# Attention and expert layer on one core: 2304-byte loads, row-tiled matmuls and a fixed matmul order

## Chip, cores, metric

One core of a Trainium2 chip. The metric is device time in microseconds (us) of one execution of the whole kernel, as the median of several runs. Each execution on record is classed as fast or slow; all that are compared below are fast, unless said otherwise.

Engines: PE does matmuls, DVE is the vector engine, ACT the scalar engine, POOL the third element-wise engine (it also issues the weight loads), SP issues loads and stores. In the kernel before, ACT and POOL issue the loads of k and v as well, and ACT one store. (In both kernels the matmuls write to PSUM and all other tiles lie in SBUF; an evacuation copies a result from the first to the second.)

## The reference, cut to what matters

```python
# q, k, v: (8 batches, 8 heads, 576 tokens, 64), fp32
q_s = softmax of q over the 64 features           # exp, row sum, divide
k_s = softmax of k over the 576 tokens
kv  = einsum('bhsd,bhse->bhde', k_s, v)           # 64 x 64 per head
x   = einsum('bhsd,bhde->bhse', q_s, kv)          # then (batch, 576, 512)
# expert layer: ONE expert per batch, out of 8
logits = x.mean(axis=1) @ w_gate                  # needs all of x of a batch
e      = argmax(logits);  gate = softmax(logits)[e]
out    = gate * (relu(x @ w1[e]) @ w2[e])         # 512 -> 1024 -> 512
```

The choice of the expert needs the mean over all tokens of a batch, so a batch's weights can be asked for only once its attention is done. Both kernels therefore run the attention two batches ahead of the expert layer ("MoE" below).

## The kernel before

The parts that the change and the argument touch:

```python
# loads: 512 tokens as 4 tokens a partition (1024-byte pieces), 64 tokens as a tail (256-byte pieces)
q_main = q[:, :, 0:SM, :].rearrange("b h (p j) d -> b p h (j d)", p=128)
q_tail = q[:, :, SM:S, :].rearrange("b h p d -> b p h d")
...
for hp in range(NP):                     # 4 pairs of heads a batch
    ... 5 transposes of q into PSUM, one copy: qt_sb[feature, token]
    ... 5 matmuls ek x v -> pa[:, 0:128];  5 matmuls ek x ones -> pa[:, 128:129]
    nc.vector.reciprocal(out=icv, in_=pa[:, 128:129])
    nc.vector.scalar_tensor_tensor(out=kv_sb, in0=pa[:, 0:128], scalar=icv, in1=blkmask, ...)
    nc.tensor.matmul(pm, lhsT=kv_sb, rhs=qt_sb[:, 0:SM], start=True, stop=True)
    nc.vector.tensor_tensor_reduce(      # the evacuation of x: PSUM fp32 -> SBUF fp16, and the sum over tokens
        out=xt[:, hp, 0:SM], in0=pm, in1=ones_f32.to_broadcast([128, SM]),
        scale=1.0, scalar=0.0, op0=ALU.mult, op1=ALU.add, accum_out=pooled[:, hp:hp + 1],
    )
    ... the same for the 64-token tail
...
# MoE: 8 hidden chunks (4 matmuls N=512, 4 of N=64, relu on ACT or DVE), then 5 output tiles
#      (8 matmuls each, scaled by gate on ACT or DVE), one store of 4 tiles and one of the tail
for b in range(B + LOOKAHEAD):
    if b < B:
        attention_and_gating(b)
    if b >= LOOKAHEAD:
        moe(b - LOOKAHEAD)
```

The softmax here doesn't subtract the row's maximum and nothing guards it: scores larger than these inputs give would overflow.

## Time and profile before

| | before |
|---|---|
| time, median | 249.94 us (249.49 to 252.18, 3 runs) |
| span of the profiled run | 248.0 us |
| PE busy, DVE busy | 194.3 us, 141.3 us |
| first MoE matmul | 54.0 us |
| one MoE without attention beside it | 17.0 us |

The prediction below shows the slices, the chain and the cost rows of this profile. One line of the page that it only quotes in part, the transfers:

```profile
DMA packets 56863, 50.03 MB, mean 202 GB/s; under 512 B 14352, under 2 KB 55312, under 8 KB 55824
```

Nearly all packets are under 2 KB and a quarter are under 512 B: that is what the change set out to improve.

### The profile page before, as it was taken

To read this page: it belongs to the slowest core of one execution; us is meant where nothing else is said; L and a number is where in the kernel's file an instruction comes from. 1 tells how busy PE (TensorE), PEld (TensorE's weight loads), DVE (VectorE), ACT (ScalarE), POOL (GpSimd) and SP (SyncE) were. 2 spreads that over 40 slices of the span, in tenths; PEclk is the share of its full clock that TensorE was granted. 3 is DMA by queue.
4 is the path that set the end of the run, shared out by engine and by line. 5 is a ranking of instruction groups with operands and counts; after the bars stand their busy time and mean duration, and the time that the engine had idled before them with its cause. 6 is when DMAs were issued, how large, how long until landed. Compare 5 with 4: busy or idle time off the path is not lost.

```text
span 248.0 us, 3617 instructions
## 1 busy us (share of the span) xinstructions
PE 194.3 (78%) x1376; PEld 100.3 (40%) x1376; DVE 141.3 (57%) x397; ACT 80.6 (32%) x106; POOL 41.1 (17%) x62
## 2 busy tenths in 40 slices
PE   0006645129954999999999999999999999999862
PEld 0004323015522554555545455554545444444321
DVE  0067998606890799698798699547465422222120
ACT  2083705004600650652651563123122322413311
POOL 2040020502040204213304021301400500000000
PEclk9999999999996899999999999999999999999999
DMA  6999999999999699999999999994894398105005
GB/s 193 249 259 298 271 286 250 269 242 205 275 273 207 113 278 244 259 233 290 271 247 204 201 299 176 155 199 181 141 206 185 48 204 237 45 0 190 0 0 190
DMA packets 56863, 50.03 MB, mean 202 GB/s; under 512 B 14352, under 2 KB 55312, under 8 KB 55824
## 3 DMA queue, kind: packets, MB, share of 16 engines
q0 software_dynamic: 29440, 21.50, 57.7%
q1 hardware_dynamic: 14224, 17.84, 22.6%
q10 hardware_dynamic: 13184, 10.49, 15.3%
q8 instruction: 10, 0.16, 0.2%
q14 instruction: 5, 0.04, 0.1%
HBM read 61.88 MB, written 9.44 MB: 288 GB/s over the span
## 4 chain that ended last, share of the span: by engine, by line
PE 60%; DMA 18%; DVE 15%; ACT 2%; issue 2%; POOLq 1%; POOL 1%; SPq 0%; DVEq 0%
PE po L277 24%; PE phm L252 19%; DMA w_sb<-in_moe_w_dram 13%; DMA qm<-in_q_dram 5%; PE pa L159 4%; DVE qs L117 4%; PE pa L145 3%; DVE eq L120 3%; DVE xt L188 3%; PE pht L257 2%; PE pa L168 2%; PE pa L163 2%; PE pm L185 2%; DVE hsb L264 1%; PE pa L150 1%
## 5 line engine op out<-in xcount | busy, mean ns | idle before, releaser
L252 PE MATMUL phm<-xt,w_sb 128*128 128x512 f16 x256 | 71.3, 392 | 16.8 <-DMA w_sb<-in_moe_w_dram 15.6
L277 PE MATMUL po<-w_sb,hsb 128*128 128x512 f16 (+1 forms) x320 | 77.8, 380 | 3.3 <-DVE osb L284 1.7
L277 PEld LDWEIGHTS <-hsb 128*128 128x128 f16 (+1 forms) x320 | 30.6, 100 | 39.5 <-issue 8.1
L262 ACT ACTIVATE hsb<-phm 128x512 f16<-128x512 f32 x32 | 19.1, 596 | 55.8 <-PE phm L252 55.5
L252 PEld LDWEIGHTS <-w_sb 128*128 128x128 f16 x256 | 21.7, 99 | 38.2 <-DMA w_sb<-in_moe_w_dram 16.7
L282 ACT ACTIVATE osb<-po,gate 128x512 f32<-128x512 f32 (+1 forms) x24 | 16.4, 684 | 63.4 <-PE po L277 63.4
L145 PE MATMUL pa<-ident,eq 128*128 128x128 f16 x128 | 14.9, 245 | 22.4 <-DVE eq L120 20.3
L264 DVE TENSOR_SCALAR hsb<-phm 128x512 f16<-128x512 f32 x32 | 22.0, 686 | 15.7 <-PE phm L252 15.4
L284 DVE TENSOR_SCALAR osb<-po,gate 128x512 f32<-128x512 f32 x16 | 12.0, 748 | 29.1 <-PE po L277 29.1
L117 DVE TENSOR_REDUCE qs<-eq 128x32 f32<-128x2048 f16 x8 | 18.2, 2276 | 14.6 <-ACT eq L108 14.6
L188 DVE CUSTOM_DVE_ANT_0 xt<-pm,ones_f 128x512 f16<-128x512 f32 x32 | 21.4, 687 | 5.8 <-PE pm L185 5.1
L178 DVE RECIPROCAL icv<-pa 128x1 f32<-128x1 f32 x32 | 5.1, 164 | 28.1 <-PE pa L172 27.9
L145 PEld LDWEIGHTS <-eq 128*128 128x128 f16 x128 | 9.5, 108 | 27.7 <-DVE eq L120 20.3
L108 ACT ACTIVATE eq<-qm 128x2048 f16<-128x2048 f32 x8 | 15.3, 1910 | 15.9 <-DMA qm<-in_q_dram 9.0
L110 ACT ACTIVATE ek<-km 128x2048 f16<-128x2048 f32 x8 | 15.2, 1904 | 11.6 <-DMA km<-in_k_dram 10.6
L120 DVE TENSOR_TENSOR eq<-eq,qsi 128x2048 f16<-128x2048 f16 x8 | 18.2, 2276 | 0.0
L98 POOL DMA_DIRECT2D vm<-in_v_dram x8 | 7.3, 910 | 63.2 <-PE pa L163 62.8
L257 PEld LDWEIGHTS <-w_sb 128*128 128x128 f16 x256 | 13.0, 101 | 8.3 <-issue 0.6
L185 PE MATMUL pm<-qt_sb,kv_sb 128*128 128x512 f16 x32 | 12.9, 423 | 4.3 <-DVE kv_sb L180 4.3
L159 PE MATMUL pa<-vm,ek 128*128 128x128 f16 x128 | 14.7, 243 | 1.5 <-DVE qt_sb L156 1.5
L156 DVE COPY qt_sb<-pa 128x576 f16<-128x576 f16 x32 | 14.0, 450 | 3.2 <-PE pa L150 3.0
L257 PE MATMUL pht<-xt,w_sb 128*128 128x64 f16 x256 | 14.7, 197 | 0.0
(52 smaller groups left out, 168.7 us busy)
## 6 DMA issues: line engine op xcount, KB each, us to landing
w_sb<-in_moe_w_dram POOLq DMA_DIRECT2D x32, 512.0 KB, 11.9
km<-in_k_dram ACTq DMA_DIRECT2D x8, 1024.0 KB, 9.9
qm<-in_q_dram SPq DMA_DIRECT2D x8, 1024.0 KB, 13.3
out_dram<-osb SPq DMA_DIRECT2D x8, 1024.0 KB, 6.2
vm<-in_v_dram POOLq DMA_DIRECT2D x8, 512.0 KB, 13.2
qtl<-in_q_dram SPq DMA_DIRECT2D x8, 128.0 KB, 11.0
ktl<-in_k_dram ACTq DMA_DIRECT2D x8, 128.0 KB, 9.5
out_dram<-osb ACTq DMA_DIRECT2D x8, 128.0 KB, 3.5
```

Source lines behind the costliest of these rows:

```text
L117: nc.vector.tensor_reduce(out=qs, in_=eq, op=ALU.add, axis=AX.X)
L120: nc.vector.tensor_tensor(out=eq, in0=eq, in1=qsi.unsqueeze(3).to_broadcast([128, 4, H, Dh]), op=ALU.mult,)
L145: nc.tensor.transpose(out=qT_ps[:, j * 128:(j + 1) * 128], in_=eq[:, j, hs, :], identity=ident,)
L159: nc.tensor.matmul(pa[:, 0:128], lhsT=ek[:, j, hs, :], rhs=vm[:, hs, j, :], start=(j == 0), stop=False,)
L185: nc.tensor.matmul(pm, lhsT=kv_sb, rhs=qt_sb[:, 0:SM], start=True, stop=True)
L188: nc.vector.tensor_tensor_reduce(out=xt[:, hp, 0:SM], in0=pm, in1=ones_f32.to_broadcast([128, SM]), scale=1.0, scalar=0.0, op0=ALU.mult, o ...
L252: nc.tensor.matmul(phm, lhsT=w1_sb[:, dc, fsl], rhs=xt[:, dc, 0:SM], start=(dc == 0), stop=(dc == ND - 1),)
L257: nc.tensor.matmul(pht[:, fc, :], lhsT=w1_sb[:, dc, fsl], rhs=xt[:, dc, SM:S], start=(fc == 0 and dc == 0), stop=(fc == NF - 1 and dc == N ...
L262: nc.scalar.activation(out=hsb[:, fc, 0:SM], in_=phm, func=AF.Relu)
L264: nc.vector.tensor_single_scalar(out=hsb[:, fc, 0:SM], in_=phm, scalar=0.0, op=ALU.max)
L277: nc.tensor.matmul(po[0:nparts, :], lhsT=hsb[:, fc, cols], rhs=w2_sb[:, fc, :], start=(fc == 0), stop=(fc == NF - 1),)
L282: nc.scalar.mul(osb[0:nparts, st, :], po[0:nparts, :], gate[0:nparts])
```

## The change

Intent: larger descriptors for q, k and v (64 partitions per head with 9 neighbouring tokens each, 9 x 64 x 4 = 2304 bytes), so no token tail in the attention; two heads side by side in the upper and lower 64 rows of PE (row tiles); the column sum of k as an extra ones column of v instead of extra matmuls; gating on one partition; and a Python generator for the attention, stepped once after each step of the MoE, which fixes the order of the matmuls by hand. The core of the diff, with cuts:

```diff
-        qm = qk_in.tile([128, H, 4 * Dh], FP32, name="qm")
-        nc.sync.dma_start(out=qm, in_=q_main[b])
-        ... k on the ACT queue, v on the POOL queue with a cast, three tails
+    def pair_src(t, b, i):
+        return t[b].rearrange("(i n g) (p j) d -> i (g p) n (j d)", i=2, n=2, p=64)[i]
+    def loads(b):
+        for i in range(2):
+            for name, t in (("q", q), ("k", k), ("v", v)):
+                nc.sync.dma_start(out=x, in_=pair_src(t, b, i))      # 2304-byte pieces
 ...
+            for j in range(J):                                       # J = 9
+                for g in range(2):
+                    r = slice(64 * g, 64 * g + 64)
+                    nc.tensor.matmul(kps[g][:, 0:129], lhsT=ek[r, j], rhs=va[r, j], ...)
 ...
-            nc.vector.tensor_tensor_reduce(
-                out=xt[:, hp, 0:SM], in0=pm,
-                in1=ones_f32.to_broadcast([128, SM]), ...
+                xo = xt[:, c, :].rearrange("q (p j) -> q j p", j=J)
+                nc.vector.tensor_tensor_reduce(
+                    out=xo[:, 0:8, :], in0=px.rearrange("q (j p) -> q j p", j=8),
+                    in1=ones_f32.unsqueeze(2).to_broadcast([128, 8, 64]), ...
 ...
-            if st % 2 == 0:
-                nc.scalar.mul(osb...)      # else on DVE
-        nc.sync.dma_start(out=out_main[b], in_=osb[:, 0:4, :])
+            osb = o_pool.tile([128, D], FP32, name="osb")            # 4 buffers
+            nc.scalar.mul(osb[0:rows], po[0:rows], gate[0:rows])
+            nc.sync.dma_start(out=out[b, st * 128:st * 128 + rows, :], in_=osb[0:rows])
 ...
+    with tc.manual_schedule(engines={ET.PE}):
+        for b in range(B):
+            att = attention(n, ins.pop(n), False)                    # n = b + 2
+            next(att)                                                # the preparation
+            for step, _ in enumerate(moe(b)):
+                next(att, None)
+            drain(att)
```

The matmuls leave x in PSUM in the order "for each j, all 64 p", where the token is 9p + j. The new `xo` puts the tokens back in order while it evacuates: neighbouring elements of the input go to places 9 fp16 elements, that is 18 bytes, apart.

## The prediction

> **What bounds the kernel now.** I read the page first (busy shares, the 40 slices, the chain, the groups), then the table of stretches, then VectorE's timeline in a dense stretch. The slices and the chain split the run in two parts:
>
> ```profile
> PE   0006645129954999999999999999999999999862
> DMA  6999999999999699999999999994894398105005
> PE 60%; DMA 18%; DVE 15%; ACT 2%; issue 2%; POOLq 1%; POOL 1%; SPq 0%; DVEq 0%
> ```
>
> A slice is 6.2 us. Until slice 12 (about 78 us) the tensor engine (PE) has holes and DMA is full; from there to the end PE is full and DMA empties out by slice 28. The chain, in order of time, names the holes: whole stretches waiting for expert weights.
>
> ```profile
> 1.34 11.52 DMA qm<-in_q_dram
> 43.33 10.60 DMA w_sb<-in_moe_w_dram
> 69.29 8.30 DMA w_sb<-in_moe_w_dram
> 115.06 14.10 DMA w_sb<-in_moe_w_dram
> ```
>
> (Start, length, what.) The first MoE matmul runs at 54 us. The stretches below give PE's work; columns are window, length, busy us and instructions of PE, weight loads, DVE, ACT, POOL, then clock, DMA share, GB/s written.
>
> ```profile
> 126.00:131.00 5.00, 4.53 (x30) 2.34 (x29) 4.92 (x15) 2.79 (x7) 0.76 (x2) 1.00 1.24 207
> 150.30:173.00 22.70, 22.18 (x169) 11.61 (x168) 14.78 (x54) 5.32 (x10) 3.79 (x6) 1.00 0.99 180
> 214.10:231.10 17.00, 16.99 (x105) 7.89 (x104) 4.30 (x7) 5.05 (x9) 0.00 (x0) 1.00 0.19 70
> ```
>
> A batch has 1376/8 = 172 matmuls, 104 of them MoE. A MoE alone takes 17.0 us (last line); with one batch of attention mixed in about 22 us (middle line). The first line is the weight stream alone: 207 GB/s written as fp16, so 414 GB/s read as fp32, with DMA engines full. Vector-engine costs come from these groups and this piece of timeline:
>
> ```profile
> L188 DVE CUSTOM_DVE_ANT_0 xt<-pm,ones_f 128x512 f16<-128x512 f32 x32 | 21.4, 687 | 5.8 <-PE pm L185 5.1
> L117 DVE TENSOR_REDUCE qs<-eq 128x32 f32<-128x2048 f16 x8 | 18.2, 2276 | 14.6 <-ACT eq L108 14.6
> L120 DVE TENSOR_TENSOR eq<-eq,qsi 128x2048 f16<-128x2048 f16 x8 | 18.2, 2276 | 0.0
> L156 DVE COPY qt_sb<-pa 128x576 f16<-128x576 f16 x32 | 14.0, 450 | 3.2 <-PE pa L150 3.0
> L264 DVE TENSOR_SCALAR hsb<-phm 128x512 f16<-128x512 f32 x32 | 22.0, 686 | 15.7 <-PE phm L252 15.4
> 107.63 0.68 DVE L264 TENSOR_SCALAR hsb<-phm 128x512 f16<-128x512 f32 x1
> 108.25 0.69 DVE L188 CUSTOM_DVE_ANT_0 xt<-pm,ones_f 128x512 f16<-128x512 f32 x1
> 108.87 0.08 DVE L188 DVE_READ_ACCUMULATOR2_ANT pooled<- 128x1 f32 x1
> ```
>
> Independent operations follow 0.62 us apart where one lasts 0.69: I use start-to-start costs.
>
> **What the Trainium skill says.** (1) "TensorE: Matmul & The Clock Gate", back-to-back issue gap: N=512 costs 215.7 ns warm. The trace agrees: 8 po matmuls in 1.73 us on the chain. (2) "TensorEngine Tiling (Array Packing)", key properties: row tiles run in parallel, but switching the mode drains the array; the kernel before has no row tiling, so its trace cannot say what the drain costs. (3) "DMA: Bandwidth & Descriptors", queues, rings and completion order: a ring is consumed in order and an engine alternates between the rings that have work. The trace before has queues 0, 1 and 10 active together, which fits; it gives no shares, so equal shares below are my assumption. (4) The same page, why small descriptors are slow: a fixed cost per packet. Here 14352 of 56863 packets are under 512 B (the 256 B tails).
>
> **The change part by part.**
>
> DMA. Bytes read from HBM are unchanged (61.88 MB). q, k and v go from 1024 B and 256 B pieces to 2304 B, all on the SP queue; v is cast on POOL. Lone load stretches before reach 320 to 360 GB/s; estimate for 2304 B: 390. All 28.3 MB of q/k/v then need 73 us, weights 33.5 MB/414 = 81 us, output 9.4 MB/390 = 24 us: 178 us. DMA alone no longer sets the end if it is fed evenly.
>
> PE per batch of attention: before 20 transposes, 20 kv, 20 column-sum and 8 x matmuls, 22 - 17 = 5 us. After: 36 transposes of N=64 (the N=64 pht matmuls run 30 ns apart: 1.1 us, or half if row tiles overlap), 36 kv of N=129 (at 56 ns 2 us, or 1), x 4 x 0.25 = 1 us, gate 0.5 us: 3 to 4.5 us. The gain is 1 to 2 us a batch, 8 to 16 us in all if PE stays the bound.
>
> Vector engine. Same elements, so the same sum, but the built program's instruction order confines it. Each batch's attention is spread over MoE steps 0 to 9: transposes after hidden chunk 0, kv after 1, x after 2 and 3, the second half at 4 to 7, gate after the first output step. DVE's static order in a half is: 2 copies, hsb, next batch's row-sum and scaling mixed with icv and kv, x evacuations, another hsb. Start-to-start: copies 0.94, hsb 2 x 0.62, row-sum and scaling 2 x 1.23 (2.18 x 1152/2048), icv, reciprocal and kv 1.0, xt 2 x 0.62, tails 0.5: 7.4 us, two halves a batch. The PE needs 4 us of hidden-chunk work per half, so DVE sets the pace of this phase. And in the output phase (5 steps of 1.73 us) DVE has almost nothing: osb moved wholly to ACT, and the next transposes come only after it. Period: 1.75 (chunk, transposes, latency) + 7.4 + 0.8 (second transposes, DVE waiting) + 5.7 (second half up to the evacuation before the last x) + 0.3 + 1.8 (first output step) + 0.6 (gate) + 7.0 = 25.4 us, against 22 before. Six such batches: 152 us, 20 us worse than before. The last two MoEs: 2 x 16.7 = 33 us.
>
> Start. q of a half is 0.59 MB and lands near 5 us instead of 12.9. Both first batches' attention is drained on PE before the first MoE. DVE in order does 7 row-sum and scaling pairs (17 us), four attention halves (4 us each), gates and waits: first MoE at about 43 us instead of 54. Its w1 starts at 28 us and, with half the bandwidth, lands at 40.
>
> A new wait. On SP, the loads of six batches (36 DMAs) stand before the first output, and ACT's fifth output tile reuses the first of 4 osb buffers. That store is behind 21.2 MB of loads in one ring, which by my account share with weights from 28 us on and finish at 80 to 88 us. The first MoE ends near 69 us; ACT, blocked on its osb, cannot evacuate the next MoE. Cost 8 to 18 us, take 14. Later stores follow few loads: none.
>
> End: osb 0.7 and store 3.5 us, as before: 4.
>
> Sum: 43 + 152 + 14 + 33 + 4 = 246. Summing latencies I did not see (mode drains, cold PE at the start) I add 2: 248 us.
>
> **The rivals.** (a) PE stays the bound: the period is 17 + 3.5 = 20.5 us, the load stall is small: 43 + 123 + 33 + 4 + 5 = 208 to 215. For it: DVE was only 57% busy, and the matmul order leaves a chunk between each producer and consumer. Against: the static DVE order, 15 us of work that must fit where PE needs 11. If the period lies between, 225 to 235. (b) The stall behind the loads is the largest: DMA is shared less kindly, the second MoE resumes at 92 us, each period takes 27 us: 262 or more. For it: DMA share is above 1 in all early stretches. Against: fewer packets. (c) DMA stays the bound: 8.9 MB a batch at 400 GB/s is 22 us, less than my period, so it would be hidden; only with a period of 20 us does it bite, and then it gives about 215. (d) POOL's v copies delay weight issues, since they stand before them in its order; weights are asked for over one period ahead, so I expect nothing after the start.
>
> **Range and chances.** My own sum is near the old time with an error of some 12 us: six times the uncertainty of the period (1.5 us) and 8 us of the stall. A rebuild with this much hand-placing suggests somebody saw matmul holes close, so I give the fast side more than the sum does: 228 to 264, faster by over 2% (under 245) 0.42, within 2% 0.31, slower 0.27.
>
> **What would show it right or wrong.** Right: the first MoE matmul at 40 to 46 us; a hole in PE of 8 us or more between 65 and 92 us with ACT's osb waiting for DMA; then a repeating pattern of 25 us with DVE nearly full for 15 us and empty for 8, PE waiting for DVE (hm, tk or x banks) in the hidden-chunk phase; two last MoEs of 16.7 us; DMA far from full after 110 us. Wrong: PE above 95% busy between 45 us and the end, a period near 20 us, or DMA landings of weights in the late chain. The load rate is wrong if q tiles land slower than every 5 us early on.

## The result

The changed kernel took 295.55 us (median of 4 runs, 294.0 to 296.1), the kernel before in the same rounds 249.72 us (248.8 to 252.18). The ratio is 1.179, with a 95% interval of 1.170 to 1.187: slower by 18%, far outside the predicted range. (Ratios here are the mean time of one kernel's fast runs over that of the other's in the same rounds, so not quite the ratio of the medians quoted.)

| | before | after |
|---|---|---|
| time, median | 249.72 | 295.55 |
| span of the profiled run | 248.0 | 292.3 |
| PE busy / DVE busy | 194.3 / 141.3 | 194.8 / 180.7 |
| first MoE matmul | 54.0 | 57.85 |
| DMA packets | 56863 | 31956 |

The page of the changed kernel: busy times, the slices (7.3 us each) of PE, DVE and DMA, the transfers, and the chain by engine.

```profile
PE 194.8 (67%) x1552; PEld 97.3 (33%) x1552; DVE 180.7 (62%) x365; ACT 91.5 (31%) x130; POOL 52.6 (18%) x73
PE   0232233294769566895969585893879675999994
DVE  2699999758870979259870979259571868030210
DMA  7999999999938996499738910497018900696112
DMA packets 31956, 54.81 MB, mean 187 GB/s; under 512 B 2752, under 2 KB 10944, under 8 KB 31936
DVE 52%; PE 42%; DMA 2%; issue 1%; ACT 1%; ACTq 1%; DVEq 0%
```

DVE's share of the chain went from 15% to 52%, and DMA's from 18% to 2%. DVE has 39.4 us more of busy time with fewer instructions. DVE runs at 7 to 9 tenths and then drops to 2, again and again; PE is full for a slice at a time only, until the last ones. (The first line gives each engine's busy us, its share of the span and its instructions.) In the groups of the page one row stands out:

```profile
L182 DVE CUSTOM_DVE_ANT_1 xt<-x,ones_f 128x512 f16<-128x512 f32 x24 | 58.8, 2449 | 2.5 <-PE tk L180 2.5
L187 DVE CUSTOM_DVE_ANT_0 xt<-tk,ones_f,pooled 128x64 f16<-128x64 f32 x32 | 15.9, 513 | 2.2
```

(Busy us and mean ns after the first bar.) This is the evacuation of x. The row of the kernel before, shown in the prediction, had the same 128x512 elements at 687 ns; now it is 2449 ns (2512 ns in the 8 that run before the first MoE), and the 64-token rest went from 278 to 513 ns. The other DVE work of the attention did not get dearer than counted, except for the relu right after the first evacuation of a half (0.83 us from start to start, 0.60 in experiment 2 below). DVE's timeline in one half of a batch's attention (start, length, what):

```profile
94.39 0.82 DVE L154 COPY qt<-tk 128x576 f16<-128x576 f16 x2 [6.69 <-PE tk L147]
...
99.23 2.39 DVE L182 CUSTOM_DVE_ANT_1 xt<-x,ones_f 128x512 f16<-128x512 f32 x1
...
101.23 0.91 DVE L254 TENSOR_SCALAR hsb<-hm 128x512 f16<-128x512 f32 x1
102.06 0.49 DVE L187 CUSTOM_DVE_ANT_0 xt<-tk,ones_f,pooled 128x64 f16<-128x64 f32 x1
...
102.25 2.54 DVE L182 CUSTOM_DVE_ANT_1 xt<-x,ones_f 128x512 f16<-128x512 f32 x1
...
104.95 0.50 DVE L187 CUSTOM_DVE_ANT_0 xt<-tk,ones_f,pooled 128x64 f16<-128x64 f32 x1
```

From the first copy to the end of the last evacuation it is 11.06 us, where the prediction had 7.4. Of this, the piece from the start of the first evacuation (99.23) to the end of the second tail (105.45) is 6.22 us. And PE waits for it (the bracket has the idle time before, and what ended it):

```profile
101.68 0.38 PE L179 MATMUL x<-qt,kv 128*128 128x512 f16 x1 [2.43 <-DVE pooled L182]
...
105.50 0.64 PE L147 MATMUL tk<-ident,eq 64*128 64x64 f16 x17 [2.31 <-DVE pooled L187]
106.07 1.89 PE L242 MATMUL hm<-xt,w_sb 128*128 128x512 f16 x4
```

The table of stretches for one repeat of the pattern, from one MoE's first matmul to the next one's (columns as in the prediction: window, length, busy us and instructions of PE, weight loads, DVE, ACT, POOL, then clock, DMA share, GB/s):

```profile
125.82:158.81 32.99, 25.57 (x195) 12.46 (x195) 22.42 (x45) 11.27 (x16) 6.23 (x8) 0.84 0.84 208
254.67:271.37 16.70, 16.70 (x106) 7.91 (x105) 2.77 (x4) 6.42 (x10) 0.00 (x0) 1.00 0.86 188
```

A batch takes 33.0 us, 16.3 us more than a MoE alone (second line). PE is idle for 7.4 us of it (32.99 - 25.57), and in the trace DVE ends every one of these holes. The clock column of 0.84 is a side effect: after the hole of 2.3 us in front of a transpose (105.50 in the timeline above), the next four 512-wide matmuls took 1.89 us instead of 1.04.

So the mechanism that the prediction chose is there (DVE's fixed order sets the pace while hidden chunks run), but one of its terms is more than three times its predicted size. Why does the same operation on the same number of elements take 3.6 times as long? Three readings:

- The step: fp16 elements written 18 bytes apart are slow to write.
- The form: a three-dimensional access pattern or this operation's variant is slow (the name ends in 1 instead of 0).
- The company: other engines or DMAs disturb the write; in the kernel before they would do less of that.

The Trainium skill has a note that bears on the first, and I had not read it before predicting: the page "SBUF — State Buffer", section "Door 1: The DMA port swizzle", speaks of 16-byte lines and says "each access that crosses to a new line pays a penalty"; it gives 8 bf16 elements as the step that is still free. A step of 9 is just past that, so the page would have warned. It names no size for the penalty.

### The profile page after: what moved, and what is told of

Same layout as the page of the kernel before. It is cut to its first block, busy times and chain, and to the rows that moved or that the text cites. A ratio compares the mean times of both kernels' runs of the same rounds, so it can differ in the third digit from the quotient of the medians.

```text
span 292.3 us, 4145 instructions
## 1 busy us (share of the span) xinstructions
PE 194.8 (67%) x1552; PEld 97.3 (33%) x1552; DVE 180.7 (62%) x365; ACT 91.5 (31%) x130; POOL 52.6 (18%) x73
## 2 busy tenths in 40 slices
DMA packets 31956, 54.81 MB, mean 187 GB/s; under 512 B 2752, under 2 KB 10944, under 8 KB 31936
## 4 chain that ended last, share of the span: by engine, by line
DVE 52%; PE 42%; DMA 2%; issue 1%; ACT 1%; ACTq 1%; DVEq 0%
DVE xt L182 25%; PE po L263 21%; PE hm L242 14%; DVE eq L134 7%; DVE qs L131 6%; DVE xt L187 5%; DVE hsb L254 4%; DMA wg_sb<-in_moe_w_gate_dram 2%; PE tk L147 2%; DVE kv L170 2%; PE ht L247 1%; PE tk L161 1%; DVE qt L154 1%; DVE qsi L133 1%; ACTq L86 1%
## 5 line engine op out<-in xcount | busy, mean ns | idle before, releaser
L242 PE MATMUL hm<-xt,w_sb 128*128 128x512 f16 x256 | 76.4, 430 | 0.0
L182 DVE CUSTOM_DVE_ANT_1 xt<-x,ones_f 128x512 f16<-128x512 f32 x24 | 58.8, 2449 | 2.5 <-PE tk L180 2.5
L254 DVE TENSOR_SCALAR hsb<-hm 128x512 f16<-128x512 f32 x32 | 24.4, 764 | 32.3 <-PE hm L242 32.0
L210 POOL DMA_DIRECT2D w_sb<-in_moe_w_dram x32 | 19.3, 623 | 109.9 <-DVE gt L224 70.7
L252 ACT ACTIVATE hsb<-hm 128x512 f16<-128x512 f32 x32 | 19.0, 593 | 61.9 <-PE hm L242 61.9
L126 POOL CAST va<-v_in 128x1152 f16<-128x1152 f32 x16 | 20.2, 1272 | 89.8 <-PE tk L161 47.8
L131 DVE TENSOR_REDUCE qs<-eq 128x18 f32<-128x1152 f16 x16 | 21.5, 1342 | 7.2 <-ACT eq L115 7.2
L120 ACT ACTIVATE ek<-k_in 128x1152 f16<-128x1152 f32 x16 | 18.5, 1159 | 17.0 <-PE tk L161 16.3
L115 ACT ACTIVATE eq<-q_in 128x1152 f16<-128x1152 f32 x16 | 18.6, 1162 | 16.3 <-PE tk L147 8.1
L134 DVE TENSOR_TENSOR eq<-eq,qsi 128x1152 f16<-128x1152 f16 x16 | 21.7, 1358 | 0.1
L247 PE MATMUL ht<-xt,w_sb 128*128 128x64 f16 x256 | 19.5, 202 | 0.0
L182 DVE CUSTOM_DVE_ANT_1 xt<-po,ones_f 128x512 f16<-128x512 f32 x8 | 18.6, 2512 | 0.7 <-PE po L179 0.4
```

What stands on the lines that cost most here:

```text
L126: nc.gpsimd.tensor_copy(out=va[:, :, 1:].rearrange("p j (n d) -> p n j d", n=2), in_=tiles["v", i].rearrange("p n (j d) -> p n j d", j=J),)
L131: nc.vector.tensor_reduce(out=qs, in_=eq, op=ALU.add, axis=AX.X)
L134: nc.vector.tensor_tensor(out=eq, in0=eq, in1=qsi.unsqueeze(3).to_broadcast([128, J, 2, Dh]), op=ALU.mult,)
L182: nc.vector.tensor_tensor_reduce(out=xo[:, 0:8, :], in0=px.rearrange("q (j p) -> q j p", j=8), in1=ones_f32.unsqueeze(2).to_broadcast([128 ...
L210: nc.gpsimd.dma_start(out=w1_sb[64 * h:64 * h + 64, 2 * i:2 * i + 2, :], in_=w1_src[i, h])
L242: nc.tensor.matmul(phm, lhsT=w1_sb[:, c, fsl], rhs=xt[:, c, 0:SM], start=(c == 0), stop=(c == ND - 1),)
```

## The experiments

### 1. The write made contiguous, rows put in order by the store (e1_contig)

```diff
-                xo = xt[:, c, :].rearrange("q (p j) -> q j p", j=J)
+                xo = xt[:, c, :].rearrange("q (j p) -> q j p", j=J)
...
-            nc.sync.dma_start(out=out[b, st * 128:st * 128 + rows, :], in_=osb[0:rows])
+            for t in range(rows // 64):      # out_jp = out.rearrange("b (p j) d -> b j p d", j=J)
+                nc.sync.dma_start(out=out_jp[b, 2 * st + t], in_=osb[64 * t:64 * t + 64])
```

The access pattern keeps its three dimensions and the operation its name; only the step of the output goes from 18 to 2 bytes. Nine stores of 64 rows a batch take the place of five.

> The changed kernel with one thing undone: xt is written with unit stride (columns in j, p order), and nine stores per batch put the rows back in token order; the result stays right. Theory 1 (the 18-byte step of the 2-byte writes is what made the x evacuations 2.45 us instead of 0.69, and nothing else of importance was mis-sized): the 512-wide evacuation falls to about 0.69 us, the tail from 0.51 to 0.28, the pattern of 33.0 us shrinks to 25 to 26.5, the first MoE matmul moves from 57.9 to 42 to 46 us, and the time is 238 to 255 us; a hole with ACT's osb waiting for a store of up to 18 us may now appear between 65 and 92 us, since the first MoE ends earlier. Theory 2 (the evacuation is slow for another reason, such as its PSUM read, its accumulator[...]): evacuations stay above 1.5 us and the time above 275 us. Theory 3 (other waits between PE and DVE are as large as the evacuations): evacuations fall to 0.69 us but the period stays above 29 us and the time above 265 us.

Measured: 249.84 us (249.4 to 249.91), before 250.05; ratio 0.997 (0.990 to 1.003). The evacuation fell to 685 to 687 ns, still under the name ending in 1. The form is thereby refuted as the cause. The first MoE started at 45.5 us, the pattern was 24.9 us, and a wait of 19.8 us of ACT for an output store appeared, which the changed kernel did not have.

### 2. The stride alone undone (e8_stride_only)

Only the first line of the diff above, with the changed kernel's own five stores. The output rows then stand in another order.

> The changed kernel with the stride of the x write alone undone, and its own two kinds of store kept (five of 128 or 64 rows a batch); the rows of the output then stand in another order, wrong on purpose. It tells whether the stall of the first contiguous run (20 us of ACT waiting for an output store) came from its nine smaller stores or from the loads that stand before any store. Theory R (loads before stores in one ring, the predicted wait): 244 to 253 us, ratio 0.98 to 1.01, one wait of ACT for an output store of 15 to 22 us at 70 to 92 us, pattern 24.5 to 25.5 us. Theory N (the nine small stores made the stall): wait under 5 us, 226 to 236 us, ratio 0.91 to 0.95. Theory S (something else than the stride made the changed kernel slow): over 270 us.

Measured: 249.35 us (248.29 to 250.0), before 250.75 (one of its seven runs is slow and not used in the ratio); ratio 0.998 (0.989 to 1.007). So one line of the change is worth 46 us (295.55 to 249.35), and the nine smaller stores of the first experiment cost nothing that these runs can resolve (249.84 against 249.35). DVE's timeline in the same half as above, ACT's at the end of the first MoE, and the stretch of one repeat:

```profile
117.10 0.82 DVE L154 COPY qt<-tk 128x576 f16<-128x576 f16 x2 [6.70 <-PE tk L147]
...
121.94 0.68 DVE L182 CUSTOM_DVE_ANT_1 xt<-x,ones_f 128x512 f16<-128x512 f32 x1
...
124.19 0.28 DVE L187 CUSTOM_DVE_ANT_0 xt<-tk,ones_f,pooled 128x64 f16<-128x64 f32 x1
```

```profile
69.23 0.69 ACT L268 ACTIVATE osb<-po,gate 128x512 f32<-128x512 f32 x1 [1.04 <-PE po L263]
90.61 0.68 ACT L268 ACTIVATE osb<-po,gate 64x512 f32<-64x512 f32 x1 [20.70 <-DMA out_dram<-osb]
```

```profile
115.55:140.45 24.90, 21.75 (x195) 10.99 (x195) 15.06 (x45) 11.15 (x16) 6.23 (x8) 1.00 1.05 275
```

From the first copy to the end of the tail it is 7.37 us, against 7.4 in the prediction and 11.06 in the changed kernel; the evacuations' own piece is 2.53 us instead of 6.22. That is 3.7 us a half, 7.4 us a batch, of the 8.1 us by which the patterns differ (33.0 and 24.9). In the second fence the fifth output tile waits 20.7 us for a buffer, whose store stands behind the loads: SP issued it at 69.3 us, and it landed at 90.5, right after the last of the loads issued before it (89.1). It is the wait that the prediction had put at 8 to 18 us. Theory R held in all its numbers.

The trace also shows what sets the repeat. PE is idle for 3.15 us of it (24.90 - 21.75), in five holes, and DVE ends all five. A repeat in which DVE has two row sums and scalings of the next batch to do takes 24.9 us, the fifth, with one of them left, 23.2, and the sixth, with none, 21.6.

A warning on correctness: the comparison with the reference passed this output too, as it passed the next experiment's, although both have their rows in another order. Its tolerance does not see the order of rows. That the versions called right below store their rows in order rests on the index argument (place 64j + p of x holds token 9p + j, and the stores undo that), not on the comparison.

### 3. The stride alone added to the kernel before (e3_before_strided)

```diff
+            xo = xt[:, hp, :].rearrange("q (p j) -> q j p", j=9)
             nc.vector.tensor_tensor_reduce(
-                out=xt[:, hp, 0:SM], in0=pm,
-                in1=ones_f32.to_broadcast([128, SM]),
+                out=xo[:, 0:8, :], in0=pm.rearrange("q (j p) -> q j p", j=8),
+                in1=ones_f32.unsqueeze(2).to_broadcast([128, 8, 64]),
```

The tail likewise; the output rows are permuted.

> The kernel before with one part of the change alone: xt is written with the same 18-byte step as in the changed kernel; the output rows are then permuted, so the result is wrong on purpose. Theory 1: the 512-wide evacuation takes 2.4 to 2.5 us and the tail 0.5, so DVE gets 32 x 1.76 + 32 x 0.24 = 64 us more work (141 to about 205 us busy); from 78 us on it had some 4 us of slack per batch of 22 us, so a period becomes 25 to 27 us and the time 265 to 295 us. Theory 2: evacuations stay near 0.7 us and the time within 2% of 249 us.

Measured: 289.0 us (288.52 to 291.94), before 250.05; ratio 1.157 (1.146 to 1.167).

```profile
L189 DVE CUSTOM_DVE_ANT_1 xt<-pm,ones_f 128x512 f16<-128x512 f32 x32 | 75.7, 2469 | 6.4 <-PE pm L185 4.5 <-PE pa L186 2.0
```

The one stride makes the old kernel 39 us slower, with none of the new loads, row tiles or orders present. Its DVE busy time rose from 141.3 to 194.3 us. The company reading is refuted with that: in another program the same write takes the same 2.4 to 2.5 us.

### 4. The write measured by itself (m1_strides)

Before the kernel's own work, four rounds of single operations on 128 x 512 elements: the evacuation operation from PSUM to fp16 at steps of 2, 4, 8, 12, 14, 16, 18 and 32 bytes, to fp32 at 4, 8, 16 and 20 bytes, plain casts on three engines, and strided reads. ACT's cast reads PSUM like the evacuation, POOL's reads SBUF.

> The kernel before (with two instead of three weight buffers to make room) and in front of it, four times each, single 512-element operations into scratch: the evacuation's operation from PSUM to fp16 at steps of 2, 4, 8, 12, 14, 16, 18 and 32 bytes, to fp32 at 4, 8, 16 and 20 bytes, plain copies at 2 and 18 bytes from PSUM and SBUF, a copy that reads at 18 bytes, ACT and POOL copies at 2 and 18 bytes. Only single durations count. Theory 1a (cost depends on the byte step[...]): 0.69 us up to 14 bytes or a gradual rise below 16, about 2.4 us at 16, 18 and 32 bytes, for fp16 and fp32 alike, and for plain copies too. Theory 1b (any non-unit 2-byte write is slow[...]): 2.4 us already at 4 bytes, fp32 at any step 0.69. Theory 2 (the three-dimensional form or the second operand of the changed kernel): all steps near 0.69 us here, because these have plain two-dimensional operands.

The groups, by step: 2, 4, 8, 12, 16, 18 bytes into fp16, then 16 bytes into fp32, then casts at 18 bytes: on DVE from SBUF, on ACT and on POOL (mean ns is the number after the comma):

```profile
L79 DVE CUSTOM_DVE_ANT_0 h<-ps,one 128x512 f16<-128x512 f32 x4 | 2.8, 692 | 9.2 <-ACT h L98 9.2
L80 DVE CUSTOM_DVE_ANT_0 h<-ps,one 128x512 f16<-128x512 f32 x4 | 2.9, 725 | 0.1
L81 DVE CUSTOM_DVE_ANT_0 h<-ps,one 128x512 f16<-128x512 f32 x4 | 5.2, 1290 | 0.1
L82 DVE CUSTOM_DVE_ANT_0 h<-ps,one 128x512 f16<-128x512 f32 x4 | 7.4, 1855 | 0.1
L84 DVE CUSTOM_DVE_ANT_0 h<-ps,one 128x512 f16<-128x512 f32 x4 | 9.7, 2422 | 0.1
L85 DVE CUSTOM_DVE_ANT_0 h<-ps,one 128x512 f16<-128x512 f32 x4 | 9.6, 2388 | 0.1
L89 DVE CUSTOM_DVE_ANT_0 f<-ps,one 128x512 f32<-128x512 f32 x4 | 4.2, 1049 | 0.1
L94 DVE CAST h<-src 128x512 f16<-128x512 f32 x4 | 5.2, 1289 | 0.1
L98 ACT CAST h<-ps 128x512 f16<-128x512 f32 x4 | 9.6, 2390 | 0.1
L99 POOL CAST g<-src 128x512 f16<-128x512 f32 x4 | 9.8, 2460 | 0.0
```

The time rises with the step and is flat from 16 bytes on (32 bytes: 2286 ns). A step of 4 bytes is nearly free, 8 bytes costs 1.9 times, 12 bytes 2.7 times, 16 bytes 3.5 times. So this is not a jump past a limit of 16 bytes: moving from 9 to 8 elements would have bought nothing. The name ending in 0 is slow too at 18 bytes, and a plain cast is (2385 against 685 ns), so it isn't the operation. ACT (586 to 2390) and POOL (617 to 2460, from SBUF) pay as much; neither would have been an escape. In fp32, 16 bytes cost 1049 ns. A read with an 18-byte step, fp16 to fp16, took 626 ns against 293. One result narrows the reading: the same plain cast on DVE at 18 bytes, but from SBUF, took 1289 ns (421 contiguous), about half of the 2385 from PSUM. So the cost is not the write's step alone; where the input lies counts too. Why that is so, and what makes the rise gradual, these runs do not show.

### 5. Ten output buffers (e4_osb10)

On top of experiment 1, `o_pool` has 10 buffers instead of 4, so that two MoEs' outputs need no store to have landed.

> The kernel with unit-stride xt, and 10 instead of 4 output buffers, so that ACT need not wait for a store that stands behind the loads of six batches. In the run before this, ACT's fifth output tile waited 19.8 us for a store at about 70 to 90 us. If that wait was the whole hole, it vanishes: 228 to 236 us, with the pattern still 24.9 us long. Rival: the hole is only a sign that DMA is full until 90 us; then PE or ACT waits for loads or weights at the same place instead, and the time stays above 242 us.

Measured: 231.59 us (230.8 to 231.65), before 249.23; ratio 0.927 (0.921 to 0.933). ACT's waits for osb no longer contain a store. The distance from the second MoE's start to the third's fell from 43.2 to 24.9 us, the length of the two repeats after it. The stall was worth 18 us.

### 6. DVE's order by hand (e5a_dve_order)

On top of 5, DVE is scheduled by hand as well as PE, and the attention's preparation (exponentials, v cast, row sum, scaling) is a function of its own, called after output steps 8 and 10 of the MoE before:

```diff
-    with tc.manual_schedule(engines={ET.PE}):
+    with tc.manual_schedule(engines={ET.PE, ET.DVE}):
...
             for step, _ in enumerate(moe(b)):
                 next(att, None)
+                if n + 1 < B and step in (8, 10):
+                    pre[n + 1].append(prep(ins[n + 1], len(pre[n + 1])))
```

With the preparation the loads of a batch, too, are issued one batch earlier in the program (not shown in the cut).

> As the one above, and the row sums and scalings of the next batch are issued on DVE in the output phase (after output steps 1 and 3, order on DVE fixed by hand) instead of between the evacuations of the hidden phase; no operation is added or taken away. If the confined DVE order sets the pattern of 24.9 us, as predicted, DVE has 4.9 us per half left against some 5.4 us of PE: PE becomes the bound, the pattern falls to 20.5 to 22 us and the time to 203 to 217 us. If the pattern is set by latencies between PE and DVE (transposes, copies, kv), it stays above 23.5 us and the time within 8 us of the run above. If DMA binds (71 MB at about 390 GB/s is 183 us plus the last batch), a time near 210 us with DMA full to 170 us shows it.

Measured: 225.39 us (223.54 to 227.05; one of the four runs is slow and not used in the ratio), before 249.23; ratio 0.900 (0.891 to 0.908). The pattern fell from 24.9 to 21.6 us, within the expected 20.5 to 22: DVE's order, and not its amount of work, made the 24.9. (The edit moves loads and exponentials as well, but PE's holes in the 24.9 us were all ended by DVE, see experiment 2.) The total fell by 6 us only, and missed the expected 203 to 217. The starts of the MoEs say why: the first one moved from 44.6 to 49.0 us, and one repeat of the six still took 25.5 us.

### 7. Relu on ACT, output tiles partly on DVE (e5_relu_act)

As 6, with all relu evacuations on ACT and output tiles 1 and 3 on DVE.

> As the one above, and all hidden evacuations on ACT, two of five output evacuations on DVE: 2.5 us less DVE work in the hidden phase per batch, 1.3 more in the output phase. If PE is already the bound, nothing (within 2 us of the run above, or 1 to 3 us worse, because exps and hidden evacuations now share ACT); if DVE still binds, up to 6 x 2 us = 12 us faster.

Measured: 225.27 us (223.84 to 226.96), ratio 0.902 (0.894 to 0.910): no difference from 6. Which of the two engines evacuates did not matter once the order was right.

### 8. ACT's order by hand (e6a_act_order)

One word: `ET.Activation` is added to the engines scheduled by hand. In 6, ACT's exponentials stood between relu evacuations of the running MoE.

> The run with DVE by hand and ten output buffers had a hole of some 26 us on the PE at 105 to 131 us, whose chain is stores of output tiles and then a k load; ACT's exponentials of the next batch stood between evacuations of hidden chunks in its order and waited for that load. Here ACT's order is by hand too: exponentials only after output steps 8 and 10, where nothing of the running MoE stands behind them. Theory L (the late load stops work of the running MoE because of the place of its exponential in ACT's order): the hole shrinks to under 10 us, time 205 to 217, ratio to the kernel before 0.83 to 0.87. Theory D (the load itself is too late, whatever ACT's order: the SP ring has stores before it, and the next batch can't start without it): the hole moves to the end of a MoE and stays 15 us or more, time 219 to 228.

Measured: 221.3 us (220.54 to 221.96), before 250.18; ratio 0.886 (0.881 to 0.891). First, a misreading of mine in the text above. The chain of run 6 has these pieces (start, length, what):

```profile
97.06 17.73 DMA out_dram<-osb
...
115.92 14.34 DMA k_in<-in_k_dram
...
131.43 0.59 ACT hsb L252
```

I had taken them for a hole of 26 us on PE. PE worked through nearly all of it: that is only how long the transfers that released the next step had been under way. ACT waited 4.7 us for this k load, and the relu behind it in ACT's order came late:

```profile
130.36 1.16 ACT L117 ACTIVATE ek<-k_in 128x1152 f16<-128x1152 f32 x1 [4.71 <-DMA k_in<-in_k_dram]
131.43 0.58 ACT L252 ACTIVATE hsb<-hm 128x512 f16<-128x512 f32 x1
```

The repeat took 25.5 instead of 21.6 us, so the cost was 3.9 us. With ACT ordered by hand that repeat takes 21.65 us, and the total fell by 4.1 us. So the cause that theory L names is right, but its time of 205 to 217 us was missed, since there were 4 us to be had and not 16 or more. Theory D's hole at the end of a MoE isn't there.

Now PE sets the pace from 49 us to the end. The stretch of one repeat, and PE's timeline around its row-tiled matmuls:

```profile
94.23:115.89 21.66, 21.13 (x196) 10.76 (x195) 16.67 (x46) 10.79 (x16) 6.24 (x8) 1.00 1.11 302
```

```profile
96.56 0.28 PE L247 MATMUL ht<-xt,w_sb 128*128 128x64 f16 x4
96.77 0.70 PE L161 MATMUL tk<-va,ek 64*128 64x129 f16 x18
97.41 1.04 PE L242 MATMUL hm<-xt,w_sb 128*128 128x512 f16 x4
98.28 0.28 PE L247 MATMUL ht<-xt,w_sb 128*128 128x64 f16 x4
98.40 0.38 PE L179 MATMUL x<-qt,kv 128*128 128x512 f16 x1
```

PE is busy for 21.13 of 21.66 us. The 18 kv matmuls of 129 columns occupy 0.64 us from start to the next start, 36 ns each. The prediction took 56 ns for one without overlap, which is what 128-column matmuls on the full array take in the trace of the kernel before, from start to start; so the two row tiles do run side by side. Four ht matmuls take 0.12 us up to a full-array matmul (98.28 to 98.40) and 0.21 us up to a row-tiled one (96.56 to 96.77): 0.09 us more on the way into row tiling. The way out costs about as much: 0.15 us from the last kv matmul to the next on the full array, against 0.056. A batch's attention costs PE 21.66 - 16.70 = 4.96 us here, about what the prediction read for the kernel before (5 us). What the row tiles saved is not to be seen in that sum, and these runs do not split up the rest.

### 9. SP's order by hand too (e6b_sp_order)

Loads are issued a batch earlier, with five input and six output buffers (ten no longer fit).

> As the run before, and SP's order by hand as well: loads of batch n+2 are issued during the MoE of batch n, with five input buffers and six output buffers (ten no longer fit). Theory D: with loads a batch earlier the hole is gone, 205 to 217 us (ratio 0.83 to 0.87), whatever the ACT order gave. Theory L: same as the ACT order alone within 2%. Theory V (the volume: 71 MB at some 390 GB/s is 183 us, and the last MoE of 17 us and the end of 4 come after the last weights): neither run goes under 200, and DMA stays full until some 160 us in both. If six output buffers are too few, the osb wait on a store comes back in ACT's waits, with 5 us or more.

Measured: 228.06 us (226.46 to 229.65), before 250.18; ratio 0.910 (0.904 to 0.917): slower than 8 by 7 us. ACT waits for output stores again, 10 times and 16.9 us in all:

```profile
ACT osb L273 <- DMA out_dram<-osb: 16.9, 10, 3.3
```

The expectation had named this possibility (a wait of 5 us or more if six buffers are too few). PE itself lost 6.1 us in three holes that ACT's osb ended, so these waits are nearly all of the 7 us. Several things were changed at once, the order of SP and with it the place of the loads, and the numbers of input and output buffers, so the run does not say which of them makes the waits. In the trace six loads stand in one block before the stores of a batch, and the stores land only after the last of them (a load at 113.95 us, then the stores from 114.69 on), as in experiment 2. Both 8 and 9 stayed above 200 us, with DMA full until some 150 us in 8 and 180 us in 9, a dip apart. Theory V had expected that; it does not show that volume is the bound, since PE is full in 8.

## Why the prediction was wrong, point by point

The prediction's own sum beside the two kernels that differ in one line:

| term | predicted | stride undone (exp. 2) | changed kernel |
|---|---|---|---|
| first MoE matmul | 43 | 44.2 | 57.85 |
| six MoEs with attention, stall included | 152 + 14 = 166 | 166.0 | 196.8 |
| last two MoEs | 33 | 33.4 | 33.4 |
| end | 4 | 4.3 | 4.2 |
| sum (span) | 246 | 247.8 | 292.3 |

- **The step that failed** is in the part on the vector engine: "Same elements, so the same sum", and from it the term "xt 2 x 0.62, tails 0.5". In the timeline of the result the first is 2.00 + 2.70 us from start to start, the second 0.19 + 0.50: 5.4 us where the prediction has 1.7. I took the duration from the row of the kernel before because the operation, the element count and the types agreed, and did not look at the output's step in the diff. Everything else followed: a half of 11.06 instead of 7.4 us, a repeat of 33.0 instead of 25.4, a first MoE at 57.85 instead of 43 (eight evacuations before it, each 2512 instead of 686 ns, are 14.6 us of DVE). Experiments 2 and 3 show the term from both sides, experiment 4 how it grows with the step.
- **Luck** is in the agreement of the sum with experiment 2. The six repeats without a stall took 147 us in experiment 5, not 152, and the stall 18 to 19 us, not 14; the two errors cancel in the 166. And the measured 295 us lies in the range of rival (b), 262 or more, without that rival's cause: no stall behind the loads occurred.
- **The mechanism** of the pattern was right: DVE's order confines the attention to the hidden-chunk phase. With the stride undone the repeat is 24.9 us; with DVE's order by hand it is 21.6. That also settles rival (a), a bound by PE: it needed DVE's order and ACT's changed, and then gave 221 us. Its 208 to 215 assumed a repeat of 20.5 us; it is 21.65.
- **The new wait** of 14 us (range 8 to 18) does not occur in the changed kernel. With the stride undone it is 20.7 us, and 18 us of time. In the changed kernel the first store is issued only at 84.2 us, when the loads before it have landed (82.7), and lands at 86.3; the fifth output tile is written at 93.0 us without a wait. The slow evacuation had already eaten the time that the wait would have taken. So removing the stride gave 46 us at first, and with the wait removed as well (experiment 5) 64.
- **The load rate** of 390 GB/s held: 389 to 393 GB/s in the early slices of the changed kernel's page. It was a guess above the 320 to 360 that the trace before shows, with no working behind it. DMA left the chain (18% to 2%), which is the intent of the change; that the faster loads alone did that is not shown, since with the stride undone it is back at 11%, for the wait on the store, and at 3% with ten buffers. It was worth nothing while DVE set the pace. Rivals (c), DMA, and (d), v copies on POOL, had no part in the changed kernel: none of PE's waits there ended with weights.
- **PE's attention** was predicted at 3 to 4.5 us a batch; where PE is the bound it is 4.96. The prediction says that the trace before can't tell what a change of mode costs. It could have been a hint: the tail matmuls of the old kernel run on 64 rows, and from the last full-array kv matmul to such a one it is 0.152 us from start to start (median of 32), against 0.056 between two on the full array.
- **The chances**: 0.42 for faster, given for the look of the rebuild rather than for the sum, was not founded on a view.

What stays open: why the write's cost rises gradually from 4 to 16 bytes, why the same write costs half as much from SBUF as from PSUM, and which of the edits of experiment 9 makes its waits.

## What to carry to other kernels

When a change keeps an operation and its element count, compare the access patterns on both sides, too: an fp16 write with a step of 16 bytes or more took 3 to 4 times as long on every engine tried, and here that one line outweighed all the gains of the rebuild. A permutation can go where it costs less: here, into the rows of a store, where it cost nothing that the runs could resolve. And judge a wait by what the engine that sets the pace lost, not by the length of the transfer that ended it; a delay elsewhere can hide a wait, which then comes back when the delay is mended.

## What the Trainium skill lacked or had wrong

- "SBUF — State Buffer" (the note on lines in "Door 1: The DMA port swizzle") calls steps of up to 8 bf16 or 4 fp32 elements free. Here fp16 written at 4 elements took 1290 ns and at 8 elements 2422 ns, against 692 at one; fp32 at 4 elements took 1049 against 692, and at 2 elements 688. Free, or nearly so (725 and 688 ns), was a step of 2 elements for both. The page gives no size for the penalty.
- I found no page with the cost of a strided write on ACT or POOL: 2390 against 586 ns, and 2460 against 617 ns, at 18 bytes. Nor did I find one that says that for such a write on DVE the source counts: at 18 bytes 2385 ns from PSUM, 1289 from SBUF.
- "TensorE: Matmul & The Clock Gate": the prediction's 215.7 ns stands in its section "Wait — 56ns, not 53.3ns?"; the section that the prediction names, "Back-to-back issue gap", has about 131 ns for a sustained stream of matmuls of N=512. Here 8 of them took 1.73 us, 216 ns each.
- "TensorEngine Tiling (Array Packing)", key properties: the parallel row tiles are confirmed (18 matmuls of 129 columns in 0.64 us), and the drain at a change of mode is stated without a size; going in took 0.09 us longer than a step on the full array, and going out about as much.
- On no page that I read: the read-out of the accumulator after the evacuation is recorded at 364 ns instead of 83 when the evacuation's output has a 16-byte step; it overlaps the operation behind it, which in the changed kernel took 0.83 us from start to start instead of 0.60.
